# Fewer projection groups ahead of the lead, and two more tiles of rows as units of the main loop

## The chip, the core and the metric

The kernel runs on one core of a Trainium2 chip. A core has a matrix engine (PE, whose weight loads have a row of their own, PEld), three engines for the other arithmetic (DVE, ACT, POOL), a queue engine that only issues transfers (SP), and 16 DMA engines. The metric is the device time of one execution in microseconds (us), the median of the runs shown. Of the two traces compared in this document each is one profiled execution, with times counted from the span's start.

## The reference, cut to what matters

```python
x = A_x                                       # 1 x 2048 x 576
g = sigmoid((x * gate_w).sum(-1, keepdims=True))
# A: 32 heads of width 18, each with its own q, k, v
q, k, v = split_heads(x @ wqkv)
a = softmax(q @ k.T * 18**-0.5) @ v  -> heads joined @ A_wo
# B: 32 heads of q, and one k and one v that all of them share
q, k, v = split_heads(x @ B_wq), x @ B_wk, x @ B_wv
b = softmax(q @ k.T * 18**-0.5) @ v  -> heads joined @ B_wo
return g * a + (1 - g) * b
```

All is float32. The kernel has 64 "heads" to work through, numbered u: u = 0 to 31 are the heads of B, 32 to 63 those of A. Each has 2048 queries and 2048 keys, so the scores of a head are 2048 x 2048.

## The kernel before

**Rows.** q and k of all heads, the shared k and v and the gate's sum are rows of one product, wall (576 x 1792) transposed times x transposed. It has `MT = 14` tiles of 128 rows by 2048 columns. Tile 0 holds the shared k (rows 0 to 17), the gate (row 18), the shared v (rows 32 to 49) and the q of the first four heads; the later tiles hold q of B and then q and k of A. Each number is split in two float32r parts, `h` (high) and `l` (what is left), and a product is formed as hh + lh + hl. So a group of 128 rows by 512 columns is 14 matmuls (`PROJ`).

**Prologue.** x comes in five pieces (two of 256 columns, three of 512) and is split by `split_x` in eight pieces of 256 columns: ACT writes the high part `xh`, DVE the low part `xl` and a correction for the last 64 rows (`last_x`). PE then forms the groups of tiles 0, 1 and 2, four each (function `project`, or `products` for a half). `leave` takes a group from PSUM: ACT copies the high part to `phl`, DVE subtracts for the low part; for tile 0 ACT also copies the whole to `pst`. The rows go to DRAM (`kq_d` for k and the first q, `qk_d` for all else), and come back to SBUF in the layout that the scores want (`first_back`, `rows_back`). All these transfers go through SP's queue in the order of the code, except the writes to `qk_d`, which POOL issues. `shared_v` turns the shared v into `vb` by a DVE transpose and four POOL transfers for each 512 columns.

**Scores and maxima.** For each 128 queries (a step M, 16 to a head) the maximum over all keys is needed first. The maximum of keys 0 to 1023 costs one pass in place of two where it is taken from differences: a matmul with the difference of two blocks of keys (`kdb`, or `keb` for keys 1024 to 2047) that ACT passes through Relu into `xd` or `xb` (op `x`), and a matmul with one block that DVE adds to it and reduces (op `y`, a custom instruction at L1122, with result in `mx`). Op `m` is a plain maximum over 512 keys (DVE, L706). `max_rows(u)` turns the maxima of a head into rows of its `qs` tile: DVE reduces and transposes, POOL (DVE for the first heads) splits, and SP writes `m_d` and reads it back. Op `s` is a matmul of 128 keys by 512 queries of scores (L742), which ACT exponentiates into `pt` (L750); a digit n stands for n steps of probabilities times values, four matmuls each into `acc` (L757).

**Lead and main loop.** PE works on two halves of its rows at a time: ops A and x use rows 64 to 127, ops B, y and s rows 0 to 63. A unit is a group of 27 half matmuls (13 of op A, 14 of op B). The *lead* computes maxima of steps 0 to 23 before the main loop begins, with the projection units of tiles 3 and 4 in between (eight units, `lead_units`; POOL adds, splits and sends each). Its order is a string of ops. The *main loop* then runs over T = 2, 10, 18, ... (eight steps of scores, that is 32 exponentials, in each block). Each block is one of several strings of ops that a time model (`Clock`) and the author fixed beforehand: `PLAIN` has no unit in it, `HALF14` one unit of 14 products, `TWO14` two. In the kernel before, blocks T = 10 to 210 hold the 32 units of A's values (`value_units`; six of those blocks, `TWICE`, hold two), T = 218 is `PLAIN`, and T = 226 to 722 hold the 63 units of rows of tiles 5 to 13, seven units of 292 columns to a tile (`row_units`). For each of these POOL cuts the piece of x (`cut_x`), splits the weights of a new tile (`next_w`) and splits and sends the result (`both`). At T = 730 (`RE`) the output projection begins. Pieces of slow work (`slow`: gates, normalisation) are called between blocks.

The engines take their instructions in the order of the code; PSUM's seven banks (`bank`) go round. Readers of one bank take their turn in the code's order too.

## Time and profile before

| | us |
|---|---|
| median of three runs (lowest, highest) | 2635.12 (2633.13, 2638.15) |
| span of the profiled execution | 2632.7 |
| PE busy | 2619.6 (99%) |
| DVE busy | 2395.2 (91%) |
| ACT busy | 2446.7 (93%) |
| POOL busy | 860.7 (33%) |

The profiled execution's own time is its span, 2632.7 us from its first instruction to its last; the median of the runs is 2.4 us more. A row of the timeline reads: start, duration, engine, line of the code, operation, output <- inputs, shapes, count, and in brackets the idle time before it with what ended it. "PE busy" counts matmuls from start to modelled end, and they overlap; so 99% says only that PE is hardly ever without one.

### The profile page before, as it was taken

The numbers are of one execution on the slowest core, as the hardware profiler recorded it, in microseconds if no ns is written. First come the engines' busy times: TensorE is split into PE (matmuls) and PEld (weight loads), VectorE is DVE, ScalarE is ACT, GpSimd is POOL, SyncE is SP. The second block draws the span as 40 slices with busy tenths as digits, with TensorE's granted clock in tenths as the row PEclk, the third lists the DMA queues.
The fourth block names the chain that finished last, engine by engine and source line by source line (L and its number), as shares of the span: only waits on it lengthen the run. The fifth ranks groups of instructions, "written<-read, shape, count | busy, mean of one in ns | idle before, by whom it ended". The sixth has DMA issues, their size and how long they took to land.

```text
span 2632.7 us, 66902 instructions
## 1 busy us (share of the span) xinstructions
PE 2619.6 (99%) x25197; PEld 1402.5 (53%) x25197; DVE 2395.2 (91%) x4575; ACT 2446.7 (93%) x4862; POOL 860.7 (33%) x1108
## 2 busy tenths in 40 slices
PE   9999999999999999999999999999999999999999
PEld 7655545545555455454554555545555544545665
DVE  6899999999999999999999999999998999999883
ACT  5999999999999999999999999999999999999887
POOL 5611000211365535643554446443310020012113
PEclk9999999999999999999999999999999999999999
DMA  8412111212343234323544344434422332233312
GB/s 255 141 58 61 36 48 56 74 52 72 97 117 112 88 98 116 116 90 93 149 133 138 119 130 148 143 116 123 141 95 76 100 97 85 63 88 123 112 56 93
DMA packets 176520, 270.43 MB, mean 103 GB/s; under 512 B 59161, under 2 KB 137705, under 8 KB 164817
## 3 DMA queue, kind: packets, MB, share of 16 engines
q1 hardware_dynamic: 159125, 211.39, 28.1%
q0 software_dynamic: 16032, 53.25, 5.5%
q8 instruction: 198, 3.24, 0.5%
q10 hardware_dynamic: 1040, 1.52, 0.2%
q14 instruction: 125, 1.02, 0.1%
HBM read 190.26 MB, written 66.90 MB: 98 GB/s over the span
## 4 chain that ended last, share of the span: by engine, by line
PE 96%; DMA 1%; POOL 1%; SPq 1%; issue 0%; ACT 0%; DVE 0%; ACTq 0%; POOLq 0%
PE acc L757 39%; PE bank L697 29%; PE bank L742 17%; PE bank L965 10%; SPq L163 1%; PE acc L769 1%; PE bank L945 1%; DMA xsh<-xT 0%; PE bank L278 0%; DMA ksb<-kq 0%; DMA ke<-pdhl 0%; POOL oacc L938 0%; POOL phl L242 0%; POOL pst L1099 0%; POOL qk L163 0%
## 5 line engine op out<-in xcount | busy, mean ns | idle before, releaser
L750 ACT ACTIVATE pt<-bank 128x512 f32<-128x512 f32 x4096 | 2145.0, 616 | 122.8 <-PE bank L742 71.3
L706 DVE TENSOR_REDUCE mx<-bank 128x1 f32<-128x512 f32 x3002 | 1885.7, 683 | 118.6 <-PE bank L742 58.1
L742 PE MATMUL bank<-qs,ksb 56*128 56x512 f32 x2688 | 906.9, 424 | 1.5 <-DMA qs<-m_d 1.5
L697 PE MATMUL bank<-ksb,qs 54*128 54x512 f32 x2270 | 806.4, 426 | 0.0
L757 PE MATMUL acc<-pt,vb 128*19 128x256 f32 (+3 forms) x6144 | 553.1, 455 | 0.0
L697 PEld LDWEIGHTS bank<-ksb,qs 54*128 54x128 f32 x2270 | 382.8, 184 | 319.8 <-ACT pt L750 191.2
L757 PE MATMUL acc<-pt,vg 128*19 128x512 f32 (+3 forms) x5952 | 535.1, 455 | 0.0
L742 PEld LDWEIGHTS bank<-qs,ksb 56*128 56x128 f32 x2688 | 441.0, 184 | 156.2 <-DVE mx L706 63.9
L742 PE MATMUL bank<-qs,ksa 56*128 56x512 f32 x1408 | 466.7, 425 | 0.0
L697 PE MATMUL bank<-ksa,qs 54*128 54x512 f32 x1232 | 438.6, 426 | 0.0
L703 DVE CUSTOM_DVE_ANT_0 junk<-bank,xb 128x512 bf16<-128x512 f32 x500 | 342.5, 685 | 29.6 <-PE bank L742 24.3
L700 ACT ACTIVATE xb<-bank 128x512 f32<-128x512 f32 x500 | 292.3, 606 | 13.8 <-PE bank L742 3.0
L697 PEld LDWEIGHTS bank<-ksa,qs 54*128 54x128 f32 x1232 | 207.8, 184 | 150.5 <-ACT pt L750 86.6
L240 POOL CAST mh<-mt 128x32 fp32r<-128x32 f32 x63 | 13.2, 210 | 827.4 <-DVE mt L715 605.3
L742 PEld LDWEIGHTS bank<-qs,ksa 56*128 56x128 f32 x1408 | 225.5, 184 | 84.2 <-DVE mx L706 31.3
L757 PEld LDWEIGHTS acc<-pt,vb 128*19 128x19 f32 x6144 | 123.1, 97 | 203.0 <-issue 169.5
L757 PEld LDWEIGHTS acc<-pt,vg 128*19 128x19 f32 x5952 | 119.7, 97 | 206.9 <-issue 180.9
L240 POOL CAST rhl<-rst 128x292 fp32r<-128x292 f32 (+2 forms) x81 | 34.0, 420 | 486.4 <-issue 304.7
L965 PE MATMUL bank<-xr,wrh 64*128 64x292 f32 (+1 forms) x1134 | 168.2, 300 | 0.0
L697 PE MATMUL bank<-kdb,qs 54*128 54x512 f32 x372 | 159.8, 429 | 0.0
L965 PEld LDWEIGHTS bank<-xr,wrh 64*128 64x128 f32 x1134 | 139.5, 186 | 2.8
L560 POOL TENSOR_TENSOR xr<-xst,xr 128x876 fp32r<-128x876 f32 (+1 forms) x63 | 130.5, 2071 | 0.0
(173 smaller groups left out, 2403.4 us busy)
## 6 DMA issues: line engine op xcount, KB each, us to landing
qs<-qk SPq DMA_DIRECT2D x366, 144.0 KB
xst<-xT SPq DMA_DIRECT2D x54, 438.0 KB
ksa<-qk SPq DMA_DIRECT2D x132, 144.0 KB
qk<-rhl POOLq DMA_DIRECT2D x54, 292.0 KB, 4.3
ksb<-qk SPq DMA_DIRECT2D x60, 144.0 KB
qk<-phl POOLq DMA_DIRECT2D x16, 512.0 KB, 5.7
onh<-oh POOLq DMA_DIRECT2D x32, 256.0 KB, 4.4
onl<-ol POOLq DMA_DIRECT2D x32, 256.0 KB, 4.8
```

The lines of the kernel that those rows point to most:

```text
L163: return (eng or nc.sync).dma_start(o, i)
L240: eng_h.tensor_copy(h, src)
L560: nc.gpsimd.tensor_tensor(x[:, 5:8, 0:n], t0, x[:, 0:3, 0:n].bitcast(F32), op=OP.subtract)
L697: nc.tensor.matmul(pm, qs[u % 3][b:b + 54, i * P:(i + 1) * P], k, start=True, stop=True)
L700: nc.scalar.activation(MX["x", u, i], pm, AF.Relu)
L703: nc.vector.tensor_tensor_reduce(junk, pm, MX.pop(("x", u, i)), 1.0, -3e38, op0=OP.add, op1=OP.max, accum_out=MX[u][:, i, c:c + 1])
L706: nc.vector.tensor_reduce(MX[u][:, i, c:c + 1], pm, axis=AX.X, op=OP.max)
L742: nc.tensor.matmul(ps, kst(u)[b:b + 56, i * P:(i + 1) * P], qs[u % 3][b:b + 56, c * 512:(c + 1) * 512], start=True, stop=True)
L750: nc.scalar.activation(pt, ps, AF.Exp, scale=SCALE)
L757: nc.tensor.matmul(acc[32 * j:32 * j + 19, a:b], v_of(u, i), PT[u, i, j][:, a:b], start=(i == 0), stop=(i == 15), skip_group_check=True)
L769: nc.tensor.matmul(acc[32 * j:32 * j + 19, 256 * half + a:256 * half + b], v_of(NU - 1, i), pt[:, x + a:x + b], start=(i == 0), stop=(i == ...
L965: nc.tensor.matmul(u.fp[op][:, 0:u.n], x[b:b + 64], y[b:b + 64], start=(n == 0), stop=(n == last))
```

## The change

- `NT` falls from 5 to 3. Ahead of the lead PE now forms six groups in place of twelve: four of tile 0 and two of tile 1. The lead's units are the other two of tile 1 and the four of tile 2 (six in place of eight).
- Tiles 3 and 4 become units of the main loop: `row_units` takes bounds, and runs first for tiles 3 to `RA - 1 = 4` (14 units, T = 10 to 114), then `value_units` (from `VA` = 130, two units in each of 16 blocks), then `row_units` for tiles 5 to 13 (from `RB` = 266, with five blocks of two units). `RE` stays at 730. Blocks T = 2, 122 and 258 are `PLAIN`.
- A group of tile 0 leaves PSUM by `leave_first`, which orders its readers anew, and five of the six groups are formed by halves of 256 columns, so that a half can start when its piece of x is split. POOL takes `last_x` from piece 2 on.
- `first_back` and `rows_back` bring the rows back in another order, and the lead's pairs stand in another order: (M0, h) = (0,0), (16,0), (0,1), (8,0), (8,1), (16,1).
- `shared_v` runs once in the lead: 16 transposes on PE and one copy by ACT.
- The lead's string of ops is new.

```diff
-NT = 5
+NT = 3
+RA = 5
...
-    def leave(mt, c, fp):
-        cs = slice(c * 512, (c + 1) * 512)
+    def high(fp):
         hl = stp.tile([P, 2, 512], F32R, name="phl", bufs=4)
         nc.scalar.activation(hl[:, 0, :], fp, AF.Copy)
-        if mt == 0:
-            st = stp.tile([P, 512], F32, name="pst", bufs=3)
-            nc.scalar.activation(st, fp, AF.Copy)
-            KD[c] = st
+        return hl
+
+    def low(fp, hl):
         nc.vector.tensor_tensor(hl[:, 1, :], fp, hl[:, 0, :].bitcast(F32), op=OP.subtract)
...
+    def leave_first(c, fp):
+        cs = slice(c * 512, (c + 1) * 512)
+        hl = high(fp)
         if c % 2:
...
+            nc.vector.tensor_tensor(d[KR], fp[KR], KD[c - 1][KR], op=OP.subtract)
+            nc.scalar.activation(dhl[KR, 0, :], d[KR], AF.Copy)
+        low(fp, hl)
+        if c % 2:
+            nc.vector.tensor_tensor(dhl[KR, 1, :], d[KR], dhl[KR, 0, :].bitcast(F32), op=OP.subtract)
+        st = KD[c] = stp.tile([P, 512], F32, name="pst", bufs=4)
+        nc.scalar.activation(st, fp, AF.Copy)
...
+    def shared_v():
+        pt = bank_tile(clk.bank("t", 0)).rearrange("p (j d) -> p j d", d=32)
+        for j in range(16):
+            nc.tensor.transpose(pt[:, j, 0:DH], KD[j // 4][ROW_VB:ROW_VB + DH, P * (j % 4):P * (j % 4) + P],
+                                ident[ROW_VB:ROW_VB + DH, ROW_VB:ROW_VB + DH])
+        nc.scalar.activation(vb[:, :, 0:DH], pt[:, :, 0:DH], AF.Copy)
...
     def first_back():
+        back(ksb, 0, SB, 0, 512)
+        back(qs[0], 1, SB, 0, 1024)
+        back(qs[0], 1, MB, 0, 1024)
         load_kd(kdb, ROW_KB)
-        back(qs[0], 1, MB, 0, 1024)
-        back(qs[0], 1, SB, 0, 1024)
-        back(ksb, 0, SB, 0, 512)
+        for b in (MB, SB):
+            back(qs[1], 2, b, 0, 1024)
...
+        F = project(0, 0, WP[0], 2)
+        REST_ROWS.append(leave_first(0, F))
+        F = project(1, 0, WP[1], 2)
+        chunk(1)
+        leave(1, 0, F)
+        F = project(0, 1, WP[0], 2)
+        REST_ROWS.append(leave_first(1, F))
+        first_back()
+        F = project(1, 1, WP[1])
+        chunk(2)
+        leave(1, 1, F)
+        F = project(0, 2, WP[0], 2)
+        split_x(6)
+        REST_ROWS.append(leave_first(2, F))
+        split_x(7)
+        F = project(0, 3, WP[0], 2)
+        REST_ROWS.append(leave_first(3, F))
+        rows_back()
+        WP.append(prep_w(W.pop(0)))
...
-    VB = 10
-    TWICE = [VB + 8 * n for n in range(6)]
-    when(2, lambda: begin_units(value_units()))
-    RB = VB + 8 * (32 - len(TWICE) + 1)
-    when(RB - 8, lambda: (early("px"), begin_units(row_units())))
-    RE = RB + 8 * 7 * (MT - NT)
+    VA = 10 + 8 * (7 * (RA - NT) + 1)
+    RB = VA + 8 * 17
+    RE = 730
+    TWICE = [VA + 8 * n for n in range(16)] + [RB + 88 * n for n in range(5)]
+    when(2, lambda: begin_units(row_units(NT, RA)))
+    when(VA - 8, lambda: (early("vx"), begin_units(value_units())))
+    when(RB - 8, lambda: (early("px"), begin_units(row_units(RA, MT))))
...
-        for mt, c in [(mt, c) for mt in range(3, NT) for c in range(4)]:
+        for mt, c in [(1, 2), (1, 3), (2, 0), (2, 1), (2, 2), (2, 3)]:
...
-               "yABABxyABABABxyABABxyABABxyAgBABxyABABxyABABxyABAsABxyABABxs"
-               "AyABxyABBYsBBBsBB"
-               "ssmsms")
...
+               "xyABABxyABABxyABxyABABxyABABxyABxyABABxyABABxyABABxyABABxyAB"
+               "ABxyABxyABByBBBBBssssssmsms")
```

**Where instructions stand now: DVE in the prologue.** Before, after the first two groups have left (L289 with `bank_187`, `bank_188`), DVE splits two pieces of x with their corrections, transposes the shared v and takes the third and fourth group:

```order
L289 TENSOR_TENSOR phl<-bank_187,phl 128x512
L289 TENSOR_TENSOR phl<-bank_188,phl 128x512
L394 TENSOR_TENSOR xl<-xs,xh 128x4x256
L398 TENSOR_TENSOR xh<-xs,xh 64x256
L394 TENSOR_TENSOR xl<-xs,xh 128x4x256
L398 TENSOR_TENSOR xh<-xs,xh 64x256
L324 STREAM_TRANSPOSE pst<-pst 32x512
L289 TENSOR_TENSOR phl<-bank_189,phl 128x512
L289 TENSOR_TENSOR phl<-bank_304,phl 128x512
```

After, with the same work between the first group and the fifth (`bank_179` is group 0 of tile 0, `bank_218` of tile 1, `bank_257` and `bank_307` groups 1 of both, `bank_332` group 2 of tile 0; the subtraction of the keys, `pd`, now reads the bank itself):

```order
L288 TENSOR_TENSOR phl<-bank_179,phl 128x512
L403 TENSOR_TENSOR xl<-xs,xh 128x4x256 x2
L288 TENSOR_TENSOR phl<-bank_218,phl 128x512
L301 TENSOR_TENSOR pd<-bank_257,pst 18x512
L288 TENSOR_TENSOR phl<-bank_257,phl 128x512
L305 TENSOR_TENSOR pdhl<-pd,pdhl 18x512
L403 TENSOR_TENSOR xl<-xs,xh 128x4x256 x2
L288 TENSOR_TENSOR phl<-bank_307,phl 128x512
L403 TENSOR_TENSOR xl<-xs,xh 128x4x256
L288 TENSOR_TENSOR phl<-bank_332,phl 128x512
L403 TENSOR_TENSOR xl<-xs,xh 128x4x256
```

The corrections and transposes have left DVE, and the splits of x stand between the groups that they feed, each behind the group before it.

**PE at the end of the lead.** Before, the first scores (L742) stand among the last unit's halves (L965) and the last maxima (L1112); here are the last three of the eight:

```order
L1112 MATMUL bank_1305<-ksb,qs_91 128x512
L742 MATMUL bank_1309<-qs_90,ksb 128x512
L965 MATMUL bank_1245<-xl,wh 128x512 x3
L742 MATMUL bank_1316<-qs_90,ksb 128x512
L965 MATMUL bank_1245<-xh,wh 128x512
L965 MATMUL bank_1245<-xh,wl 128x512
L742 MATMUL bank_1328<-qs_90,ksb 128x512
L742 MATMUL bank_1332<-qs_90,ksb 128x512
```

After (scores L734, units L957, maxima L1106):

```order
L1106 MATMUL bank_1095<-ksb,qs_91 128x512
L957 MATMUL bank_1045<-xl,wh 128x512 x3
L957 MATMUL bank_1045<-xh,wh 128x512
L957 MATMUL bank_1045<-xh,wl 128x512
L734 MATMUL bank_1110<-qs_90,ksb 128x512
L734 MATMUL bank_1114<-qs_90,ksb 128x512
L734 MATMUL bank_1118<-qs_90,ksb 128x512
L734 MATMUL bank_1122<-qs_90,ksb 128x512
L734 MATMUL bank_1126<-qs_90,ksb 128x512
```

All eight scores have moved behind the last unit. The pair that completes head 0's maxima, after which `max_rows(0)` runs, is the 40th of the lead's 47, where it was the 32nd.

More of the change, by code (lines that the diff above doesn't have):

```diff
@@ L253, in load_w @@
     def load_w(mt, rest=None, main=None):
-        st = wpool.tile([P, NKT, P], F32, name="wst", bufs=5)
+        st = wpool.tile([P, NKT, P], F32, name="wst", bufs=3)
         load5(st, wall[mt], rest, main)
@@ L263, in gated_mix_kernel @@
     KD = {}
-    late = []
     def project(mt, c, w, parts=1):
@@ new lines, in leave_first, with rest @@
+        if c % 2 == 0:
+            dma(tk[:, 0:2], hl[KR])
+            dma(tk[:, 2], hl[KR, 0])
+        else:
+            td = kd_d[KR] if c == 1 else ke_d
+            dma(td[:, 0:2, :], dhl[KR])
+            dma(td[:, 2, :], dhl[KR, 0])
+        def rest():
+            if c % 2:
+                dma(tk[:, 0:2], hl[KR])
+                dma(tk[:, 2], hl[KR, 0])
+            dma(z_d[cs], st[ROW_G:ROW_G + 1, :])
+        dma(qk_d[:, REST, cs].rearrange("a p f -> p a f"), hl[REST], nc.gpsimd)
@@ L349, in rows_back @@
             back(qs[0], 1, b, 1024, S)
-        dma(z, z_d.rearrange("(p f) -> p f", p=P))
-        for x in (0, 1024):
-            back(ksb, 0, MB, x, x + 512)
+        for f in REST_ROWS:
+            f()
         for b in (MB, SB):
-            back(qs[1], 2, b, 0, S)
+            back(qs[1], 2, b, 1024, S)
         for b in (SB, MB):
@@ L358, in rows_back @@
             dma(ksb[b + 54:b + 56, :], ones_r)
+        for x in (0, 1024):
+            back(ksb, 0, MB, x, x + 512)
+        dma(z, z_d.rearrange("(p f) -> p f", p=P))
         for b in (MB, SB):
             back(qs[2], 3, b, 0, S)
+    REST_ROWS = []
     with tc.tile_pool(name="xs", bufs=1, side="right") as xsp:
@@ L414, in gated_mix_kernel @@
         x0, xh = XS[0], X["h"][:, :, 0:256]
-        ST = [W.pop(0) for _ in range(3)]
+        ST = [W.pop(0) for _ in range(2)]
         WP = [main_w(ST[0])]
@@ L509, in open_ph2 @@
         L["kds"] = [p2.tile([P, 512], F32R, name="kda"), kdb]
-        early("vx")
+        early("pa")
         for t in L["ks"][:2]:
@@ L580, in row_units @@
         cut_x(0)
-        W = {NT: next_w(NT)}
+        W = {M0: next_w(M0)}
         yield
-        for mt in range(NT, MT):
+        for mt in range(M0, M1):
             rs = slice(mt * P, (mt + 1) * P)
@@ L1086, in gated_mix_kernel @@
     pos = {"s": 0, "P": 0, "x": (LEAD + 2) // 2, "y": (LEAD + 2) // 2}
-    pairs = {"x": [(M, h) for M0 in range(0, LEAD + 2, 8) for h in range(2) for M in range(M0, M0 + 8)][:-1]}
+    pairs = {"x": [(M, h) for M0, h in ((0, 0), (16, 0), (0, 1), (8, 0), (8, 1), (16, 1))
+                   for M in range(M0, M0 + 8)][:-1]}
     pairs["y"] = list(pairs["x"])
@@ L1113, in lead_max @@
         if what == "x":
-            MX["x", M, h] = lead.tile([P, 512], F32, name="xb", bufs=2) if M > LEAD else \
+            MX["x", M, h] = lead.tile([P, 512], F32, name="xb", bufs=2) if (M, h) == (LEAD, 1) else \
                 xdp.tile([P, 512], F32, name="xd", bufs=4)
@@ L1119, in lead_max @@
             MX[u] = mxs[u]
-        junk = lead.tile([P, 512], BF16, name="junk", bufs=1) if M > LEAD else \
+        junk = lead.tile([P, 512], BF16, name="junk", bufs=1) if (M, h) == (LEAD, 1) else \
             xdp.tile([P, 512], BF16, name="junk2", bufs=3)
@@ L1244, in gated_mix_kernel @@
             emit(TWO14, 2)
-        elif VB <= T < RB - 8 or RB <= T < RE:
+        elif 10 <= T < RE and T + 8 not in (VA, RB):
             emit(HALF14, 1)
```

119 lines of the change are left out of this document (29 added, 90 removed).

## The prediction

> **What bounds the kernel now.** I read the page first, then the windows over the exponentials block by block, then the timeline of the start engine by engine, and last single groups and windows for prices.
>
> ```profile
> span 2632.7 us, 66902 instructions
> PE 2619.6 (99%) x25197; PEld 1402.5 (53%) x25197; DVE 2395.2 (91%) x4575; ACT 2446.7 (93%) x4862; POOL 860.7 (33%) x1108
> ```
>
> PE is never long without work, DVE and ACT are a tenth behind. A kernel with three engines that full gains from a removed wait only where one of them stands still, and pays for work that is moved where that work ends up. So two prices are wanted: what the start gives, and what the main loop asks for 14 more units. The second can be read. ACT's exponentials count the steps, 32 to a block; these stretches lie from the first exponential of a block to that of another (the columns that matter are length and ACT's count):
>
> ```profile
> core 0: us, PE busy (x) PEld busy (x) ACT busy (x), PEclk, DMA share, GB/s
> 136.36:219.62 83.26, 33.81 (x356) 7.21 (x352) 69.35 (x128) 1.00 0.19 59
> 259.47:628.63 369.16, 164.44 (x1824) 36.38 (x1824) 317.43 (x610) 1.00 0.18 52
> 628.63:647.33 18.70, 8.87 (x120) 2.51 (x120) 16.59 (x33) 1.00 0.37 101
> 647.33:1873.64 1226.31, 545.26 (x6048) 120.72 (x6048) 1050.84 (x2018) 1.00 0.40 118
> ```
>
> Four `TWO14` blocks take 83.26, 20.81 each; 19 `HALF14` blocks with values 369.16, 19.43 each; the `PLAIN` block 18.70; 63 `HALF14` blocks with rows 1226.31, 19.46 each. A block costs more the more units it has, so PE's order, not ACT or DVE, sets the pace there, and no unit is free. The start, PE's rows, then ACT's, then DVE's:
>
> ```profile
> 22.87 1.09 PE L278 MATMUL bank<-xh,wh 128*128 128x512 f32 x4
> 48.37 0.39 PE L278 MATMUL bank<-xh,wl 128*128 128x512 f32 x1
> 48.69 1.20 PE L965 MATMUL bank<-xh,wh 64*128 64x512 f32 x8
> 54.37 0.49 PE L1112 MATMUL bank<-kdb,qs 54*128 54x512 f32 x1 [0.95 <-DVE mx L1122]
> 88.73 0.49 PE L742 MATMUL bank<-qs,ksb 56*128 56x512 f32 x1 [1.47 <-DMA qs<-m_d]
> ```
>
> ```profile
> 10.37 0.42 ACT L423 ACTIVATE xh<-xsh 128x256 fp32r<-128x256 f32 x1 [0.26 <-DMA xsh<-xT]
> 12.00 1.27 ACT L388 ACTIVATE xh<-xsh 128x1280 fp32r<-128x1280 f32 x1 [0.81 <-DMA xsh<-xT]
> 17.76 2.43 ACT L388 ACTIVATE xh<-xs 128x1280 fp32r<-128x1280 f32 x2
> 20.09 0.59 ACT L284 ACTIVATE phl<-bank 128x512 fp32r<-128x512 f32 x1
> 49.97 0.73 ACT L250 ACTIVATE wh<-wst 128x640 fp32r<-128x640 f32 x1
> 51.08 1.57 ACT L1116 ACTIVATE xd<-bank 128x512 f32<-128x512 f32 x3
> 89.26 0.60 ACT L750 ACTIVATE pt<-bank 128x512 f32<-128x512 f32 x1 [1.54 <-PE bank L742]
> 96.38 3.74 ACT L750 ACTIVATE pt<-bank 128x512 f32<-128x512 f32 x7
> ```
>
> ```profile
> 19.06 1.23 DVE L394 TENSOR_TENSOR xl<-xs,xh 128x1024 fp32r<-128x1024 f32 x1 [0.47 <-ACT xh L388]
> 37.83 0.67 DVE L305 TENSOR_TENSOR pd<-pst 18x512 f32<-18x512 f32 x1
> 50.73 0.82 DVE L251 TENSOR_TENSOR wl<-wst,wh 128x640 fp32r<-128x640 f32 x1
> 51.48 0.68 DVE L289 TENSOR_TENSOR phl<-bank,phl 128x512 fp32r<-128x512 f32 x1
> 53.61 0.69 DVE L1122 CUSTOM_DVE_ANT_0 junk<-bank,xd 128x512 bf16<-128x512 f32 x1 [1.46 <-POOL mx L492]
> 54.23 0.69 DVE L1122 CUSTOM_DVE_ANT_0 junk<-bank,xd 128x512 bf16<-128x512 f32 x1
> 79.24 0.22 DVE L713 TENSOR_REDUCE m<-mx 128x16 f32<-128x64 f32 x1
> 79.49 0.21 DVE L715 STREAM_TRANSPOSE mt<-m 128x32 f32<-128x32 f32 x1
> 91.97 0.69 DVE L1122 CUSTOM_DVE_ANT_0 junk<-bank,xd 128x512 bf16<-128x512 f32 x1
> ```
>
> PE works through eight whole groups from 22.87 to 48.76, 3.24 each, with no wait in them; ACT reaches the first Relu of the lead at 51.08, DVE its first `y` at 53.61; the first score is at 88.73 and the ninth exponential, where block T = 2 begins, at 96.38. That time is what the change can move. From T = 730 on (1873.64 here) nothing differs.
>
> **The main loop's bill.** Before, T = 2 to 722 are 83 `HALF14`, 6 `TWO14` and 2 `PLAIN`; after, 67, 21 and 3. The units of rows stand for values in 16 early blocks. So 15 x 20.81 + 18.70 = 330.9 come in, and 20 x 19.43 + 63 x 19.46 become 67 x 19.46, 310.8 less: **+20.1**. The four blocks quoted lie inside one run of values, and I allow about 1 us either way for the ends of runs and for rows in place of values (19.3 to 21.3). This is the work that PE no longer does ahead of the loop, and nothing in the loop hides it. POOL must cut x and send rows for each unit:
>
> ```profile
> 666.86:686.27 19.41, 19.41 (x191) 9.93 (x187) 18.28 (x34) 18.59 (x39) 11.27 (x14) 1.00 0.34 104
> 645.51 0.72 POOL L240 CAST wrh<-wrst 128x640 fp32r<-128x640 f32 x1
> 646.30 1.56 POOL L242 TENSOR_TENSOR wrl<-wrst,wrh 128x640 fp32r<-128x640 f32 x1
> ```
>
> In that row block POOL is busy 11.27 of 19.41, so what it does for one unit is hidden, and a second unit, in the five blocks that have two of rows, finds 8.1 us free and the time of its neighbours; were that not enough, PE would wait for the rest in each of the five. One place has no such cover: in the last of the five, T = 618, the second unit is the first of a new tile, and its weights are split (0.72 + 1.56) only when the unit before has left. At most 2.3, 0 if the ops between the two units cover it; nearer to nothing, since three groups of ops stand there: +0.5. Row units begin at T = 10, as the values did. Their loads reuse the lead's memory and so wait on SP until the lead's last rows have been sent, at about 79 by the steps below; the first unit is wanted half way into T = 10, at about 104.
>
> **The start, step by step** (times after are estimates, made of the rows above).
> - *Piece 1 of x.* ACT began its split at 12.00, released by the landing. Its transfer now stands ahead of tile 1's weights, and tile 2's come later. Between 9.5 and 12.00; I take 10.3, when the rest of piece 0 had landed (10.37).
> - *Group 0.* Split 1.27, DVE 1.23 and the correction, PE's last few: complete at 13.7. Tile 1's group follows on PE, 3.24, to 17.0.
> - *Group 1 of tile 0.* ACT meanwhile writes the high part, 0.60; DVE's low part, 0.69, and then ACT's `pst`, 0.60, follow in turn, since they read one bank; then two splits, 2.43: 18.05. DVE's part 1.23, PE's last few: complete at 20.65.
> - *Group 2.* Group 1 leaves by 0.60 + 0.67 (`pd`) + 0.69 + 0.60, ACT free at 23.3; pieces 4 and 5 are split at 25.8, by DVE at 27.05; complete at 28.3. Tile 1's second group lies in between on PE.
> - *Group 3.* High, low, `pst`, and only then piece 7's split, to 31.5; DVE to 32.75; PE done at **33.5**.
> - *To the lead.* This group leaves by 2.55, then tile 2's weights, ACT 0.73 and DVE 0.82: first Relu 36.7, first `y` **37.65**, 16.0 ahead of 53.61.
>
> The five groups after the first are 16.2 of PE's work behind 13.7, so 3.6 of the 33.5 are waits for pieces of x; before, a dozen groups covered these. The corrections moved to POOL, behind its transfers, are done before DVE's parts. The rows' way through DRAM is under this: the keys' difference is sent at 24 and, by twice the 2.92 that one hop takes below (82.35 to 85.27), back by 31; `keb` goes out at 36.3 and is wanted by the 17th pair at 48. If either takes more than its margin of 5 us, the lead waits for the rest.
>
> The lead: 47 pairs and six units are 256 half matmuls, 0.116 each (48.69: eight in 1.20, the last 0.39 long), 0.63 of PE per pair; DVE 0.62 (53.61 to 54.23); ACT 59 copies at 0.485 (51.08: three in 1.57), 0.61. Three engines within 3% and seven banks: I take 0.65, from 0.62 to 0.70. What is taken from DVE and POOL ahead of the lead (transposes, value transfers) gains nothing beyond these steps, in which neither is the last to finish; `vb` is wanted only by the first values of T = 2. Added in the lead: 16 transposes on PE. Nearest row, 16 others near the kernel's end:
>
> ```profile
> L1019 PE MATMUL bank<-ident,on 128*18 128x128 f32 x16 | 2.1, 272 | 0.0
> ```
>
> 2.1 together, part of it hidden by banks that are full: it is in the 0.65. [...]
>
> `max_rows(0)` follows the 40th pair: 37.65 + 40 x 0.65 = 63.65, DVE's two steps 0.45, 64.1. Then
>
> ```profile
> 81.77 0.22 POOL L240 CAST mh<-mt 128x32 fp32r<-128x32 f32 x1
> 82.08 0.24 POOL L242 TENSOR_TENSOR mh<-mt,mh 128x32 fp32r<-128x32 f32 x1
> 82.35 0.34 SPq L163 DMA_DIRECT2D m_d<-mh  x1
> 85.27 1.25 SPq L163 DMA_DIRECT2D qs<-m_d  x2
> 115.84 0.34 SPq L163 DMA_DIRECT2D m_d<-mh  x1
> 117.31 1.23 SPq L163 DMA_DIRECT2D qs<-m_d  x2
> ```
>
> Before, POOL began 2.07 late (79.70 to 81.77), busy with a unit. Now the unit before ends 34 ops, 4 us, ahead of that pair, and I take no wait (2.1 as the bound). POOL 0.55; from SP's issue to the first score 6.38 (82.35 to 88.73); in the main loop the first hop took 1.47 rather than 2.92, so 4.9 is the other end: 5.7. First score at 70.4. Only seven pairs and the unit's rest, 5 us, cover these nine: **PE stands some 4 us**, where before it was 1.5. All eight scores are behind that wait; ACT then needs 0.53 (88.73 to 89.26), eight at 0.485, a Relu and the gates' two, which have moved here: T = 2 at 75.7, 20.7 before 96.38.
>
> **Sum.** -20.7 + 20.1 + 0.5 = -0.1, on the profiled 2632.7; the median of the runs is 2.4 more, and the sum goes on that: 2635.0. The ends: -2.8 (9.5; 0.62; 4.9) and -0.8 in the loop; +1.7, +2.0, +2.1, +0.7 and in the loop 3.0. The 0.2% that a measurement of this kernel can tell from no change is 5.3 us.
>
> **Rivals.**
> - *The waits for x go.* PE's groups close up by the 3.6 and the rows' way through DRAM is at its short end with DVE never idle (2.0): 2629.4, or less. For it: PE's work fills only 16.2 of 19.8. Against: ACT, in the code's order, copies each group between two splits.
> - *The lead keeps its old pace*: slower. From 53.61 to 92.66 a pair took 0.83. At that pace the 40th pair is 7.2 later: 2642.2. For it: banks, ACT, DVE and PE all at their limit. Against: before, 6.6 halves stood to a pair, 0.76 of PE; now 5.4. It decides from 0.785 on (5.3 / 40 + 0.65).
> - *The clock falls in the wait of 4 us.* PE would run slowly once the scores come. In this trace the longest standstills (0.95 at 54.37, 1.47 at 88.73) left it whole:
>
> ```profile
> 80.00:90.00 10.00, 8.53 (x71) 6.56 (x68) 7.47 (x24) 7.97 (x16) 8.85 (x11) 1.00 0.43 148
> ```
>
>   At half speed for as long as it stood, 4 us, PE would fall 2.0 behind: 2637.0, the same side. [...]
> - *SP holds the maxima of head 1.* They stand behind the weights of tile 4, which wait for POOL to split tile 3's. If POOL is 6 us later than I think, PE waits at T = 16: +3, 2638.
>
> **How the numbers follow.** No change as forecast, with the clock's case 0.10 of it: 0.60. The waits go: 0.18. Old pace 0.14, SP or POOL holding the loop so long that it shows 0.08: slower 0.22. The range reaches to both first rivals, 2629 to 2642.5; the likeliest case's own is 2631 to 2639.
>
> **What would show it.** Ninth exponential at 73 to 79; first `y` near 37.6; PE's done with whole rows at 33.5; a standstill of 3 to 6 us ahead of the first score; blocks of 20.8 and 19.45, and T = 2 to 730 in 1797 to 1800 rather than 1777.26. Wrong, if a block of two row units costs over 21.5, if the 40 pairs take less than 23 or over 31 us, or if the first Relu comes before 34 or after 40.

## The result: 0.55% slower, and the profile after

| us | before | after | forecast |
|---|---|---|---|
| median (lowest, highest) | 2634.97 (2633.13, 2638.15) | 2649.14 (2647.61, 2653.55) | 2635.0 |
| span of the profiled execution | 2632.7 | 2645.8 | 2632.6 |
| ninth exponential (T = 2 begins) | 96.38 | 81.43 | 75.7 |
| T = 2 to T = 730 | 1777.26 | 1805.25 | 1797.9 |
| T = 730 to the end | 759.06 | 759.14 | unchanged |

The ratio of the times is 1.0055, 95% interval 1.0042 to 1.0068. The change is slower, by 13.1 us in the profiled executions, where -0.1 was forecast; the medians differ by 14.2 (the median of before is here that of four runs, and the profiled execution of after is the fastest of its four). The start gained 15.0 rather than 20.7, and the main loop cost 28.0 rather than 20.6. The page of the changed kernel shows little of it:

```profile
span 2645.8 us, 67415 instructions
PE 2625.2 (99%) x25371; PEld 1412.3 (53%) x25371; DVE 2392.7 (90%) x4571; ACT 2448.1 (93%) x4864; POOL 948.4 (36%) x1195
```

PE is busy 5.6 us longer though the span grew by 13.1: it now stands somewhere. The start, from the timeline of after (PE, then ACT, then DVE):

```profile
12.63 0.39 PE L277 MATMUL bank<-xh,wh 128*128 128x256 f32 x1 [3.43 <-DVE xh L407]
14.36 1.05 PE L277 MATMUL bank<-xh,wl 128*128 128x256 f32 x4
59.33 1.18 PE L331 MATMUL bank<-ident,pst 18*128 18x18 f32 x16
76.41 0.93 PE L734 MATMUL bank<-qs,ksb 56*128 56x512 f32 x3 [1.18 <-DMA qs<-m_d]
...
11.71 0.42 ACT L429 ACTIVATE xh<-xsh 128x256 fp32r<-128x256 f32 x1 [4.36 <-DMA xsh<-xT]
12.03 1.25 ACT L397 ACTIVATE xh<-xsh 128x1280 fp32r<-128x1280 f32 x1
16.68 0.60 ACT L284 ACTIVATE phl<-bank 128x512 fp32r<-128x512 f32 x1 [2.77 <-PE bank L277]
40.45 2.05 ACT L1110 ACTIVATE xd<-bank 128x512 f32<-128x512 f32 x4
...
41.41 0.68 DVE L1116 CUSTOM_DVE_ANT_0 junk<-bank,xd 128x512 bf16<-128x512 f32 x1
69.90 0.22 DVE L705 TENSOR_REDUCE m<-mx 128x16 f32<-128x64 f32 x1
```

ACT takes group 0 at 16.68 (13.7 was forecast), the first `y` is at 41.41 (37.65), and the maxima of head 0 are complete at 69.90 (63.65). So the start was 3.0 late after its first group, 3.8 late at the first `y`, 6.2 late at the 40th, and stayed so. Some blocks of the main loop (length, busy time by engine, granted clock, DMA): T = 2 and 10, the sixteen double blocks of values, T = 266, and T = 2 to 730.

```profile
81.43:101.35 19.92, 19.92 (x186) 9.31 (x184) 17.55 (x34) 18.20 (x38) 11.19 (x12) 0.92 0.44 127
101.35:121.46 20.11, 20.11 (x191) 9.70 (x187) 19.08 (x36) 18.68 (x38) 7.19 (x9) 1.00 0.42 125
393.21:726.13 332.92, 332.92 (x3295) 187.07 (x3288) 302.18 (x576) 304.98 (x609) 59.19 (x85) 1.00 0.22 67
745.24:770.39 25.15, 22.06 (x206) 12.58 (x198) 18.39 (x35) 19.06 (x39) 11.66 (x15) 0.93 0.54 149
81.43:1886.68 1805.25, 1801.89 (x17409) 939.76 (x17407) 1679.76 (x3185) 1702.26 (x3386) 791.66 (x980) 1.00 0.36 107
```

The sixteen doubles take 20.81 each, to the hundredth what four of them took before. T = 266, the first double block of rows, takes 25.15, of which PE stands 3.1; T = 2 takes 19.92 for 18.70, T = 10 20.11 for 19.46. Those three are 6.2 of the 8.3 by which the loop exceeds its 91 blocks at the forecast's prices (20.81, 19.46, 18.70). And the clock column, 1.00 in every row shown of before, is below 1 twice. Windows laid on its falls, after (length, PE's busy time and matmuls, granted clock, DMA):

```profile
9.63:13.04 3.41, 0.41 (x2) 1.00 1.05 311
13.04:16.45 3.41, 3.21 (x15) 0.50 1.05 278
33.52:36.93 3.41, 1.93 (x13) 1.00 0.92 319
74.48:77.89 3.41, 2.23 (x12) 1.00 0.48 166
77.89:84.72 6.83, 6.81 (x25) 0.50 0.29 100
760.56:763.97 3.41, 1.37 (x16) 1.00 0.50 119
763.97:767.38 3.41, 3.41 (x23) 0.50 0.99 296
```

The clock is halved three times, to 0.50 for 13.65 us in all (and once more at the very end, as before: 0.50 over the last 2.0 us there, the last 1.0 here). The second and third fall lie 64.85 and 750.93 us behind the first, 19 and 220 times 3.413, and ahead of each of the three lies a stretch of 3.41 in which PE stood for part of the time. The stretch 33.52 to 36.93, in which PE stood as well, was not followed by a fall.

### The profile page after: what moved, and what is told of

It reads as the page before. It is cut to its first block, busy times and chain, and to the rows that moved or that the text cites. A ratio compares the mean times of both kernels' runs of the same rounds, so it can differ in the third digit from the quotient of the medians.

```text
span 2645.8 us, 67415 instructions
## 1 busy us (share of the span) xinstructions
PE 2625.2 (99%) x25371; PEld 1412.3 (53%) x25371; DVE 2392.7 (90%) x4571; ACT 2448.1 (93%) x4864; POOL 948.4 (36%) x1195
## 3 DMA queue, kind: packets, MB, share of 16 engines
q10 hardware_dynamic: 1040, 1.52, 0.2%
## 4 chain that ended last, share of the span: by engine, by line
PE 96%; DMA 1%; POOL 1%; issue 0%; SPq 0%; DVE 0%; ACT 0%; ACTq 0%; POOLq 0%; DVEq 0%
PE acc L749 38%; PE bank L689 28%; PE bank L734 18%; PE bank L957 11%; PE acc L761 1%; PE bank L937 1%; PE bank L1106 0%; DMA m_d<-mh 0%; SPq L163 0%; DMA xst<-xT 0%; DMA qs<-m_d 0%; POOL oacc L930 0%; POOL wrl L242 0%; DVE junk L1116 0%; POOL xr L552 0%
## 5 line engine op out<-in xcount | busy, mean ns | idle before, releaser
L742 ACT ACTIVATE pt<-bank 128x512 f32<-128x512 f32 x4096 | 2153.9, 616 | 143.3 <-PE bank L734 77.1
L734 PE MATMUL bank<-qs,ksb 56*128 56x512 f32 x2688 | 916.2, 425 | 4.3 <-DMA qs<-m_d 4.3
L689 PE MATMUL bank<-ksb,qs 54*128 54x512 f32 x2270 | 821.5, 427 | 0.0
L749 PE MATMUL acc<-pt,vb 128*19 128x128 f32 (+3 forms) x6064 | 552.0, 460 | 0.0
L749 PE MATMUL acc<-pt,vg 128*19 128x256 f32 (+3 forms) x5936 | 534.6, 456 | 0.0
L734 PEld LDWEIGHTS bank<-qs,ksb 56*128 56x128 f32 x2688 | 443.9, 185 | 167.1 <-DVE mx L698 65.6
L734 PE MATMUL bank<-qs,ksa 56*128 56x512 f32 x1408 | 467.9, 425 | 0.0
L734 PEld LDWEIGHTS bank<-qs,ksa 56*128 56x128 f32 x1408 | 225.8, 184 | 84.7 <-DVE mx L698 31.7
L240 POOL CAST rhl<-rst 128x292 fp32r<-128x292 f32 (+2 forms) x95 | 40.0, 421 | 552.7 <-issue 378.6
L240 POOL CAST mh<-mt 128x32 fp32r<-128x32 f32 x63 | 13.2, 210 | 614.6 <-DVE mt L707 506.6
L957 PE MATMUL bank<-xr,wrh 64*128 64x292 f32 (+1 forms) x1386 | 202.9, 300 | 0.0
L957 PEld LDWEIGHTS bank<-xr,wrh 64*128 64x128 f32 x1386 | 169.7, 187 | 3.1
L552 POOL TENSOR_TENSOR xr<-xst,xr 128x876 fp32r<-128x876 f32 (+1 forms) x77 | 159.4, 2070 | 0.0
```

Source lines behind the costliest of these rows:

```text
L240: eng_h.tensor_copy(h, src)
L552: nc.gpsimd.tensor_tensor(x[:, 5:8, 0:n], t0, x[:, 0:3, 0:n].bitcast(F32), op=OP.subtract)
L689: nc.tensor.matmul(pm, qs[u % 3][b:b + 54, i * P:(i + 1) * P], k, start=True, stop=True)
L734: nc.tensor.matmul(ps, kst(u)[b:b + 56, i * P:(i + 1) * P], qs[u % 3][b:b + 56, c * 512:(c + 1) * 512], start=True, stop=True)
L742: nc.scalar.activation(pt, ps, AF.Exp, scale=SCALE)
L749: nc.tensor.matmul(acc[32 * j:32 * j + 19, a:b], v_of(u, i), PT[u, i, j][:, a:b], start=(i == 0), stop=(i == 15), skip_group_check=True)
```

## The experiments

Every kernel here is the changed kernel with the edit shown; the times stand beside its 2649.14 and beside 2634.1 to 2635.4 for the kernel before on the same chips. The intervals of the ratios reach about 3 us either way, so a verdict on less than that rests on the traces. Each trace is one execution.

**The clock: PE's standstills filled.** My theory was that the halved clock is a main cost, the rival that it lies beside other waits.

```diff
 # e1, in project(), behind the first half of group 0
+    for _ in range(7): nc.tensor.matmul(warm[:, 0:304], ident, <vb>, ...)
 # e5: the same behind the twelfth of that half's fourteen products
 # e2, at the end of the lead's string ("f" on all 128 rows)
-"ABxyABxyABByBBBBBssssssmsms"
+"ABxyABxyABByBBBBBffffssssssmsms"
```

> Seven warm-up matmuls more (14 rows of PE) between the two halves of the first group, where PE stands 3.4 us in the changed kernel; their result is not used. Theory (the clock): that standstill is what puts the granted clock to 0.50 for 3.4 us, 13.0 to 16.5. Filled, the clock stays at 1.00, the first group is complete at about 15.0 rather than 16.7, the first Relu comes at about 38.8 rather than 40.45, the ninth exponential at 79.8 rather than 81.43, and the time is 1.7 us less, about 2647.4. Rival (x): the splits of x and the order of ACT set these dates, PE's slow stretch lies beside them: the ninth exponential stays within 0.4 of 81.4 and the time within 0.5.

2650.22: a miss of the edit. PE's standstill is ahead of the last two products of the half, not behind them, so the fillers only came on top:

```profile
13.17 0.39 PE L280 MATMUL bank<-xh,wh 128*128 128x256 f32 x1 [3.48 <-DVE xh L410]
13.52 3.74 PE L274 MATMUL bank<-vb,ident 128*128 128x304 f32 x14
```

It still showed one thing: group 0 was taken at 18.97, 2.3 later (0.5 of that because the rest of piece 0 came later, at 12.25), and the first Relu came at 43.12, 2.7 later. Here group 0 does set the dates of the start.

> The same seven warm-up matmuls (14 rows of PE, 3.4 us) as in the run that filled the start, but now ahead of the first group's two products with the last 64 rows of x, where PE really stands from 9.2 to 12.6. Theory (the clock): filled there, the clock stays at 1.00 from 13 to 16.5, the first group is complete at 15.0 rather than 16.7, and since every later date of the start hangs on that group by ACT's order, the first Relu comes at 38.8 rather than 40.45 and the time is some 1.7 us less, 2647.4. Rival: the fillers only move the near-empty stretch of 3.4 us to another wait of the start (27 to 37), the first Relu comes no earlier than 40.0 and the time stays within 0.7 us.

2649.56. The clock stayed whole until 78.9, but the first Relu came at 40.03, 0.4 earlier. The fillers began late in that execution (10.58, after a late piece 0) and ran past the landing that they were to cover. Where they fitted (8.57 to 11.92, in the run with four edits below), ACT took group 0 3.9 us after it began to split the rest of piece 0; in the changed kernel that is 5.0 (11.71 to 16.68). It is 3.9 in e7 as well (11.28 to 15.19), which has no fillers and whose clock happened to stay whole there. So the slow clock costs the start about 1 us, not 1.7.

> Four fillers of PE (512 and 256 columns each, on all 128 rows, into acc, whose contents are not used at that point) between the last maxima of the lead and the first scores, where PE stands 1.2 us in the changed kernel. Theory (the clock): the near-empty stretch of 3.4 us around that wait, with ten half-height matmuls in it, is what puts the clock to 0.50 for 6.8 us. Filled, the clock stays at 1.00, the blocks T = 2 and T = 10 take 18.8 and 19.5 rather than 19.92 and 20.12, the ninth exponential comes some 1.4 us earlier, and the time is about 3.2 us less, 2645.9. Rival: these blocks are slow because DVE, ACT and the late gates delay them, and the slow clock lies beside that: T = 2 and 10 stay above 39.5 together, and the time within 1 us.

2647.52, and the blocks T = 2 and T = 10:

```profile
81.77:100.50 18.73, 18.54 (x184) 8.99 (x176) 17.54 (x34) 18.09 (x38) 10.12 (x11) 1.00 0.46 125
100.50:121.47 20.97, 20.22 (x191) 9.77 (x187) 20.02 (x36) 18.68 (x39) 8.21 (x10) 1.00 0.42 122
```

The clock is whole and T = 2 at its forecast price, as the theory wanted; but T = 10 takes up 0.9, and T = 18 begins at 121.47 as in the changed kernel (121.46). What T = 2 gained was lost in T = 10. All the traces together show what either block depends on. T = 2 goes with the time at half speed within it:

| run | e2, e13 | e9 | after, e14 | e1 | e3 | e6 | e8 | e7 |
|---|---|---|---|---|---|---|---|---|
| at half speed in T = 2, us | 0 | 1.5 | 3.3 | 3.8 | 4.1 | 4.5 | 5.4 | 9.7 |
| T = 2, us | 18.7 | 19.0 | 19.9 | 20.7 | 20.8 | 21.0 | 21.4 | 23.3 |

The six traces left out, with 4.8 to 6.4, took 21.0 to 21.4. Each us at half speed costs 0.2 to 0.5 there, mostly 0.4 to 0.5, and little ahead of it: from the first score to the ninth exponential it is 5.02 in after, with 3.5 us at half speed, 5.03 in e2, with none, and 5.33 at most. T = 10, always at full speed, goes with the time that DVE takes for the two small steps that split the maxima of head 1 (L240 and L242):

| run | e1, e3, e5, e6, e7, e8, e10 | e14 | e4 | after | e15 | e9 | e2 | e11 | e13 |
|---|---|---|---|---|---|---|---|---|---|
| DVE's two steps, us | 0.37 | 0.57 | 0.59 | 0.85 | 1.18 | 1.59 | 1.73 | 1.88 | 2.70 |
| T = 10, us | 19.6 to 19.7 | 19.82 | 19.84 | 20.12 | 20.43 | 20.83 | 20.97 | 21.12 | 21.94 |

T = 10 is 19.25 and these steps, to within 0.02 us in all but e8 (0.06) of the fifteen. They take 0.37 where POOL stands and more where POOL cuts x or splits weights beside them. In e2, T = 2 ended at 100.50 rather than 101.35, and the steps fell beside POOL's longest piece.

**The lead's pace: values turned later.**

```diff
-"...ABxyvABABxy..."  "...ByBBBBBssssssmsms"
+"...ABxyABABxy..."   "...ByBBBBBvssssssmsms"
```

> The sixteen transposes of the shared values and their copy move from the middle of the lead into the wait ahead of the first scores. Theory (the lead's pace): the transposes hold PE for 1.2 us and DVE waits 1.3 us behind them, nothing hides them in the lead: 40 pairs take 27.1 rather than 28.3 us, and as the wait ahead of the first score is as long as they are, the ninth exponential comes 1.2 us earlier, 80.2, and the time is 2647.9. Rival: the seven banks or ACT set the pace of 0.71 us to a pair, the hole only lets them catch up: 40 pairs stay at 28.0 to 28.4 and the ninth exponential at 81.4. If the slow clock after the lead also goes (transposes fill the gap), up to 3.2 us more are gained.

2647.94. The 40 pairs took 27.57 rather than 28.37, although the clock was at half for their first 1.9 us (to 43.56). With a whole clock they take 28.34 to 28.37 in six traces with the transposes among them (after, e1, e2, e5, e6, e14), and 26.97 and 27.12 in the two without (e8, e11). So the transposes cost 1.2 to 1.4, all of their 1.18 and a little more. The rest of the pace is ACT and DVE themselves. Windows over the 40 pairs, after:

```profile
41.41:69.71 28.30, 28.25 (x223) 21.00 (x224) 26.14 (x81) 25.78 (x51) 15.69 (x16) 1.00 0.58 177
```

ACT needs 25.78 for 51 instructions, 0.505 each, DVE 26.14 for 40 pairs, 0.653 (with 0.9 for tile 2's weights); 0.485 and 0.62 were forecast. What the edit gained was lost again in the first hop of the maxima, 5.33 rather than 2.40.

**The first hop of the maxima.** `m_d` is written, and only then read into `qs`. In after (SP's issues):

```profile
65.00 0.68 SPq L163 DMA_DIRECT2D qs<-kq  x2
71.00 0.35 SPq L163 DMA_DIRECT2D m_d<-mh  x1
73.40 1.25 SPq L163 DMA_DIRECT2D qs<-m_d  x2
```

In ten other traces that keep the two reads ahead of it the hop took 2.22 to 5.92. Two suspects were tried: POOL's write of the unit before, and the two reads.

```diff
 # e6, in lead_units(): the fourth unit's write waits for the fifth unit
+LATE.append((<rows of qk_d>, hl))
+if (mt, c) != (2, 1):
+    while LATE: dma(*LATE.pop(0), nc.gpsimd)
 # e9: the third head's queries move from rows_back() behind max_rows(0)
-for b in (MB, SB): back(qs[2], 3, b, 0, S)
...
     if (M, h) == (15, 1):
         max_rows(0)
+        for b in (MB, SB): back(qs[2], 3, b, 0, S)
```

> The write of the lead's fourth unit (512 KB, issued by POOL 2 us ahead of the maxima of head 0) waits until the fifth unit is split. Theory (the write): in every run so far the first hop of the maxima through DRAM ended 0.2 to 0.5 us after the landing of that write, so the hop is as long as the write ahead of it leaves it; without it 1.5 us (as in the main loop) rather than 2.4, first score at 75.5 and ninth exponential at 80.5 rather than 81.4. Rival: the hop is long by itself in the lead; it stays at 2.4 or more and the ninth exponential at 81.4.

2647.72, and the hop took 4.54: the write is not it. The theory fell.

> The two reads that bring the queries of the third head (54 rows of 8192 B, 442 KB each, issued by SP at 65.0 and 65.4 in the changed kernel) are issued behind the maxima of head 0 instead of ahead of them. Theory (the read): these reads run at 0.57 of the DMA engines from 65.5 to 72 and the 256 B packets of the maxima queue behind them; that, and not the unit's write, makes their first hop 2.2 to 5.9 us in the nine traces so far. With the reads behind, the hop takes 1.5 to 1.8, the first score comes at 74.5 to 75.5 whatever the phase, PE stands under 1 us, and the ninth exponential comes at 79.5 to 80.5; median 2646 or less. Rival: some other traffic holds the maxima; the hop stays over 2.2 and the ninth exponential at 81.4 or later.

2647.47. The hop:

```profile
73.03 0.35 SPq L163 DMA_DIRECT2D m_d<-mh  x1
74.55 1.24 SPq L163 DMA_DIRECT2D qs<-m_d  x2
75.84 0.86 SPq L163 DMA_DIRECT2D qs<-kq  x2
```

1.52, and 1.51 to 1.52 in the four later runs that keep this edit, against 2.22 or more in each of the eleven without: in this kernel the reads are the cause. The first score was still late here (77.33), since this execution was slow ahead of it (clock at half for 6.8 us up to 19.05 and for 3.4 at 42.9; first Relu at 41.17, 40 pairs in 29.7).

**T = 266.** SP's issues there, after:

```profile
745.20 2.92 SPq L163 DMA_DIRECT2D wrst<-wall  x3
748.22 0.53 SPq L163 DMA_DIRECT2D r_d<-sm  x1
748.79 3.67 SPq L163 DMA_DIRECT2D R<-r_d  x8
752.57 0.34 SPq L163 DMA_DIRECT2D m_d<-mh  x1
759.78 1.25 SPq L163 DMA_DIRECT2D qs<-m_d  x2
```

POOL had split head 17's maxima by 746.1. SP sent them at 752.57, behind the next tile's weights (held until POOL had split this tile's, to 745.2) and the eight broadcasts of a normalisation; the hop then took 7.2, and PE stood 3.1 for `qs` until 762.60. Two edits pull this apart:

```diff
 # e7: the second normalisation begins eight steps later
-when(16 * (last_head(t) + 1) + 5, ...)
+when(16 * (last_head(t) + 1) + (13 if t == 1 else 5), ...)
 # e4: rows begin at T = 274, one block of values fewer is double
-RB = VA + 8 * 17
-TWICE = [VA + 8 * n for n in range(16)] + [RB + 88 * n for n in range(5)]
+RB = VA + 8 * 18
+TWICE = [VA + 8 * n for n in range(15)] + [RB + 80 * n for n in range(6)]
```

> The second normalisation begins eight steps later, so that its sums and its broadcast come behind the maxima of T = 266 in SP's order; nothing else moves. Theory (SP's queue): SP sends these maxima at 746 to 749 rather than 752.6 and their first hop is not behind 1 MB of broadcast, so the block T = 266 takes 20.8 to 21.5 rather than 25.15, the clock stays at 1.00 there, and the time is about 4 us less, 2645. Rival (POOL and the weights): SP is held at 745.2 by the weights of the next tile, which wait for POOL, and the maxima are late anyway: the block takes 23.5 or more.

2645.58 (2645.06 to 2647.86), 3.6 less. SP's issues and the block T = 266:

```profile
750.44 2.47 SPq L163 DMA_DIRECT2D wrst<-wall  x3
753.00 0.53 SPq L163 DMA_DIRECT2D r_d<-sm  x1
753.63 0.37 SPq L163 DMA_DIRECT2D m_d<-mh  x1
755.12 1.25 SPq L163 DMA_DIRECT2D qs<-m_d  x2
756.42 3.09 SPq L163 DMA_DIRECT2D R<-r_d  x8
```

```profile
106.78:1886.66 1779.88, 1779.88 (x17227) 928.68 (x17223) 1661.54 (x3151) 1683.78 (x3350) 778.71 (x967) 1.00 0.36 107
750.28:770.57 20.29, 20.29 (x206) 11.62 (x198) 18.40 (x35) 18.54 (x39) 8.05 (x12) 1.00 0.67 146
```

With only the broadcast behind the maxima the hop takes 1.49 and the block 20.29; POOL and the weights, which still stand ahead of the maxima, cost the block nothing. And with it the whole loop from T = 10 to 730 takes 1779.88, where the forecast gives 1779.1 (1777.26 - 18.80 for T = 2, + 20.6). In e1 and in e14 below, which keep this wait, the clock happened to stay whole at it: PE stood 1.8 and 2.5, and the block took 22.29 and 23.07. So of the 4.9 by which the changed kernel exceeds e7, 2.0 to 2.8 come with a wait of that length alone; the rest is the longer wait (3.1) and the half clock together, which no run here separates.

> The rows of tiles 5 to 13 begin one block later (T = 274): one of the sixteen double blocks of values becomes two single ones, and one block of rows more is a double one, so the numbers of blocks are the same. Theory (SP's queue): in the changed kernel the start of the row units, the normalisation's broadcast and the maxima of the next head meet at T = 266, and SP sends these maxima late behind the other two; at T = 274 no maxima are due, so the block of 25.15 us goes, T = 258 to 290 take 4.3 us less, the clock stays whole there, and the time is 2644.8. Rival (POOL): a block that holds two row units, the first of them the first of all, costs 25 us wherever it stands, since POOL has to split weights and two pieces of x in it: the block T = 274 takes 23 to 25 and the time stays.

2664.26, 15 us more. At the place itself the theory held: the block T = 274, again the first double one of rows, took 20.31. But all later units now stand elsewhere against the heads:

```profile
766.41:786.72 20.31, 20.31 (x206) 11.59 (x198) 18.39 (x36) 18.55 (x39) 15.06 (x17) 1.00 0.61 183
1519.04:1546.85 27.81, 22.52 (x189) 10.55 (x187) 18.60 (x37) 18.86 (x38) 6.80 (x10) 0.88 0.42 125
1587.30:1613.93 26.63, 22.67 (x191) 10.49 (x187) 18.44 (x34) 18.71 (x38) 19.04 (x25) 0.87 0.36 121
```

T = 578 and T = 602, single blocks, cost 15.5 more than their price. In the first DVE stands 5.3 us for the sums of a normalisation, with the steps of the maxima behind it in its order; in the second PE stands 4.0 for `qs`.

**The start's order.**

```diff
 # e10
 split_x(6)
+split_x(7)
 REST_ROWS.append(leave_first(2, F))
-split_x(7)
 # e14
+W.append(load_w(1, nc.gpsimd))
 load_x(1, nc.gpsimd)
-W.append(load_w(1, nc.gpsimd))
```

> The last piece of x is split ahead of the copies of group 2, where ACT stands idle for 1.4 us in the changed kernel, rather than between them. Theory (ACT's order): PE's wait of 1.45 us at 33.5 goes, the last group is complete at 36.0 rather than 37.4 and the first Relu comes at 39.0 rather than 40.45; 1.4 us less in the end, 2647.7. Rival: DVE takes the low part of that piece ahead of group 2's, the bank and the keys' difference come later, and the first Relu stays above 40.

2650.23. PE's wait at 33.5 went, and group 3 was taken 19.0 after group 0, where it was 20.7; but the clock was at half for 6.8 us at 12.4 and again for 3.4 at 39.7, and the first Relu came at 40.68. The time says nothing, but the trace shows the next wait: PE now stood 3.6 us, until 39.82, for `kdb`, the difference of the keys on its way back from DRAM. Here is that way, its write by SP and PE's first matmul with it, in after and then in e15 (below):

```profile
26.64 1.59 SPq L163 DMA_DIRECT2D kd<-pdhl  x2
37.50 0.49 PE L1106 MATMUL bank<-kdb,qs 54*128 54x512 f32 x1 [0.20 <-DMA kdb<-kd]
...
25.54 1.47 SPq L163 DMA_DIRECT2D kd<-pdhl  x2
39.12 0.76 PE L1111 MATMUL bank<-kdb,qs 54*128 54x512 f32 x1 [5.02 <-DMA kdb<-kd]
```

In after it takes 10.9 us and ends as PE is done with its groups. In the five runs that split piece 7 early (e10, e11, e13, e15, e16) it takes 11.6 to 13.6, and PE stands 3.0 to 5.6 us for it. No run tries to shorten it.

> The weights of tile 1 are requested ahead of piece 1 of x again, as in the kernel before; nothing else differs from the changed kernel. Theory (shared transfers): the DMA engines are saturated from 7 to 23 us, so a piece requested earlier lands no earlier but puts back what shares the engines with it: the rest of piece 0 is split at 10.4 to 10.9 again rather than 11.7, piece 1 still at about 12.0; PE stands 1 us less ahead of the last two products of the first half, and the first Relu comes at 39.5 to 40.5. Rival: the spread of 10.9 to 12.8 is chance from run to run and has nothing to do with the order; the rest of piece 0 is split at 11.4 or later.

2647.14. The rest of piece 0 was split at 11.55, piece 1 at 11.88: as without the edit. The order of the requests is not what made piece 0's rest late.

**Together.**

```diff
 # e8 = e5 + e6 + e7 + "vffff" ahead of the first scores
 # e11 = e5 + e7 + e3 + e9 + e10;  e13 = e11 with "vffff"
 # e15 = e11, but without e5's fillers: e14's order, and the first half of
 #       tile 1's first group formed where they were, its weights split earlier
 # e16 = e15, and the maxima of head 1 split by POOL
-max_rows(..., nc.gpsimd if T > 16 else nc.vector)
+max_rows(..., nc.gpsimd if T > 2 else nc.vector)
```

> All of these together: fillers in the right place of the start, values turned behind the last maxima with four fillers behind them, the fourth unit's write later, the second normalisation later. If the terms add up: 1.7 of the start's clock, 0.8 of the lead's pace, 1 to 3 of the first hop, 4 of T = 266, so 2640 to 2642 with the ninth exponential at 77.5 and the clock whole from 17 us on. If the waits are in the shadow of each other (the first row units' load and POOL set T = 18), the ninth exponential is earlier but T = 10 takes longer by as much, and the time is 2644 or more.

2643.14. The 40 pairs took 26.97 and T = 266 20.32; the hop took 5.92, the clock fell for 13.65 us, and the ninth exponential came at 81.96.

> Together: fillers in the right place of the start, values turned behind the last maxima, second normalisation later, third head's queries read behind the maxima, last piece of x split early. If the terms add up against the run with four of the edits (2643.1, first hop 5.9 us): 4 us of the hop and 1 to 3 us of the slow clock in T = 2 that follows from the wait, 1.4 of the split: 2635 to 2638, with the first Relu at 37.3, the ninth exponential at 76 to 77 and T = 2 at 18.7 to 19.5. If the first row units (their load and POOL) set T = 18, then T = 10 grows by as much and the time stays above 2640.

2642.90 (2639.52 to 2644.86; the trace is of the fastest). `kdb` came at 37.46, the first Relu at 38.02, the ninth exponential at 77.55, but T = 2 and T = 10 took 42.5 together, with the clock at half from 73.7 to 83.9.

> The same with four fillers of PE behind the transposes, ahead of the first scores. If the clock still falls without them, T = 2 and T = 10 together are 1 to 2 us shorter with them and the time 1 to 2 us less; if the short hop has already closed the wait, they delay the first score by up to 1 us and the time is the same or 1 us more.

2642.07. The clock stayed whole there and T = 2 took 18.73; T = 10 took 21.94, 2.70 of it DVE's two steps. `kdb` came at 39.08 and the first Relu at 39.82.

> The old order of requests, and the first half of tile 1's first group formed in the gap in which PE waits for the rest of x (useful work in place of fillers); with it the values turned late, the second normalisation later, the third head's queries read behind the maxima and the last piece split early. Theory: PE keeps its clock in the start, the first group is complete at 14.5 to 15, the first Relu at 36.8 to 37.6, the ninth exponential at 76 to 77.5, and the time is 2640 to 2642, 1 us less than with fillers. Rival: the splits of tile 1's weights on ACT and DVE now stand ahead of piece 1's and put it back; the first Relu stays at 38 or later and the time at 2643.

2643.81. Group 0 was taken at 15.58 and group 3 at 34.19, 3.2 earlier than in the changed kernel, but PE then stood 5.0 for `kdb`, and the first Relu came at 39.98. So whether the half group is better than fillers stays open.

> The same, and the maxima of head 1 (T = 10) are split by POOL rather than by DVE. In the traces so far DVE took 0.7 to 2.2 us for these two small steps while POOL cut x beside it, against 0.43 on POOL. Theory (POOL beside DVE): without them on DVE the block T = 10 takes 19.5 to 20.3 rather than 20.8 to 21.9 where T = 2 is short, and the time is about 1 us less than the run without this edit. Rival (POOL's queue): POOL reaches them only behind its second piece of x, at 103, so the maxima go out no earlier and T = 10 stays at 20.8 or more.

2640.84 (2638.82 to 2643.83), ratio to before 1.0022, interval 1.0013 to 1.0031. DVE's two steps in e15, then POOL's in e16 (the transpose ends at 102.5 in both):

```profile
102.56 0.44 DVE L240 CAST mh<-mt 128x32 fp32r<-128x32 f32 x1
103.03 0.74 DVE L242 TENSOR_TENSOR mh<-mt,mh 128x32 fp32r<-128x32 f32 x1
```

```profile
102.64 0.21 POOL L240 CAST mh<-mt 128x32 fp32r<-128x32 f32 x1 [1.96 <-DVE mt L712]
102.93 0.25 POOL L242 TENSOR_TENSOR mh<-mt,mh 128x32 fp32r<-128x32 f32 x1
102.59:122.04 19.45, 19.45 (x191) 9.94 (x187) 18.40 (x34) 18.59 (x38) 11.22 (x14) 1.00 0.45 137
```

T = 10 takes 19.45, its price, where e15 took 20.43 after the same T = 2 (21.42 and 21.44). So what T = 10 waited for was DVE's time for the split of the maxima beside POOL's cutting of x, as expected; POOL now takes the maxima ahead of that piece, so its queue was no obstacle. The date at which the maxima leave has no part in it: SP sent them at 105.52 here and at 104.58 in e15. By the traces the edit is worth 0.9 us at T = 18; the rest of the 3.0 between the two medians is not explained by it. This is the best version found. It does not beat the kernel before.

## Why the prediction was wrong, step by step

Two terms of the start were mis-sized, group 0 and the lead's pace, and the main loop had waits that the bill put at nothing. Two of the three signs that the prediction named for being wrong came: the first Relu after 40 (40.45) and a block of two row units over 21.5 (T = 266, 25.15).

- **Group 0 (13.7; measured 16.7): mis-sized by 3.0.** I took 10.3 for piece 1, "when the rest of piece 0 had landed (10.37)". The rest itself came at 11.71, and at 10.9 to 12.8 in the fifteen other traces, so piece 1's split began at 12.03, as in the kernel before (1.7 of the 3.0). The other 1.3 is mostly the half clock, about 1 (e7, e8). Why the rest lands later than in the one trace of before stays open; the order of requests was tried (e14) and is not it.
- **From there to the first `y`: 0.8 late**, the order of ACT as forecast. That PE's groups wait for pieces was right. One size behind it was wrong without a cost here: the keys' difference, which I had sent at 24 and back by 31, took 10.9 rather than 7 and came at 37.50, just as PE was done. In e10 and the four runs built on it, it is what PE waits for.
- **The lead's pace (0.65; measured 0.71): mis-sized by 2.4 over 40 pairs.** ACT's 0.505 for a copy and DVE's 0.653 for a pair leave 0.674 even without the transposes (e8), 1.0 of the 2.4. The other 1.4 is the transposes, which I had put "in the 0.65". They took 1.18 together, less than the 2.1 of my row, but nothing hid them.
- **The way of the maxima (6.75 from the 40th pair to the first score; measured 6.6): right**, POOL without a wait included, but by luck: the hop is 2.2 to 5.9 as the two reads of `qs` fall, and 1.5 without them. The shorter lead brought them closer: they are issued 6.0 us ahead of the maxima (65.00, 71.00), in the kernel before 9.9 (72.48, 82.35). The 2.92 of that kernel, from which I worked, had its own cause, which stays open.
- **PE's standstill (4 us; measured 1.2)** was a slip of the working: its own terms give 6.7 from the 40th pair to the first score, and 5 of cover leave 1.7. The "nine" holds the 2.1 of POOL's wait that the sum left out. In the other traces PE stands there for 0 to 4.2. The clock's rival had one of the three places. That the clock falls in a wait of 4 us was my assumption, which no row of before shows; here it was at 0.50 behind a standstill of 1.18. The rival's price, half of the time at half speed, was an assumption too and comes near what T = 2 paid (1.2 for 3.3 us); the 3.5 us ahead of T = 2 cost nothing.
- **The main loop's bill (+20.1): right.** Sixteen doubles at 20.81; e7's loop from T = 10 on is 0.8 off. The 0.5 for T = 618 was 0.18.
- **What the bill left out: 7.4.** The rival "SP holds the maxima" had the mechanism, but I looked for it at T = 16 alone and gave it, with POOL's, 0.08. It came at T = 266 (+4.3, e7 removes it). T = 2 is +1.2, the half clock. T = 10 is +0.7, DVE's split of the maxima beside POOL's `cut_x` (e16 removes it); I had seen that POOL has time for its work, and not that DVE is slower beside it (its two steps took 0.37 to 2.70). The kernel before had this too, beside POOL's work for values: 1.06 for the two steps, and 21.19 for its T = 10 where a double block costs 20.81. Of the other 1.2, 0.7 lie in T = 122 and T = 258, `PLAIN` blocks that took 19.02 and 19.11 rather than 18.70; the remainder, over 86 blocks, stays open.

So 3.8 + 2.4 - 0.4 in the start and 7.4 in the loop make the 13.2 between forecast and measurement. The median is another 0.9 above the forecast, which no trace shows. I had weighed the mishaps one at a time, and they came together; even all the upper ends that the sum names (1.7, 2.0, 2.1, 0.7 and 3.0) would give only 2644.5.
